# A fused attention and gated-convolution kernel: fewer tiles turned on TensorE, one store of 1/z, another order of the steps

## The chip, the cores and the metric

The kernel runs on one core of a Trainium2 chip. The metric is device time in microseconds (us), the median of several runs. Engines are called as in the profile: PE (TensorE, matmul), PEld (its weight loads), DVE (VectorE), ACT (ScalarE), POOL (GpSimd), SP (SyncE, which here issues every DMA).

## What is computed

Two layers follow each other. The first is attention of 4 batches of 12288 queries (C = 128 channels) on 768 keys that are pooled from a 384 x 32 image by 4 x 4 means and projected; keys and values are the same. The second is a causal convolution with 5 taps, a sigmoid, and two 128 x 128 projections.

```python
kv_pool = kv.reshape(B, H // r, r, W // r, r, C).mean(axis=(2, 4))
k = v = kv_pool.reshape(B, -1, C) @ w_sr
s = (1 / sqrt(C)) * (q @ k.T);  s = s - s.max(-1)
a = exp(s);  a /= a.sum(-1) + 1e-09;  x = a @ v
...
gate_pre[t] = sum(conv_w[k] * x_padded[t + k] for k in range(5))
out = (sigmoid(gate_pre) * (x @ w_val)) @ w_out
```

## The kernel before

The 4 x 12288 queries are cut into 96 groups of 512 (24 groups for each batch), and a group into 4 tiles of 128 queries (j = 0 to 3). Each group goes through these steps; names are the tiles of the profile.

Scores: for each tile six matmuls (L445) give `s` (128 x 768) from a high and a low half of q (`qh`, `ql`) and of the keys (`kh`, `kl`). DVE takes the row maximum (`nm`, L457), ACT the exponential with its row sum in `z` (L471). The result is needed with keys on the partitions, as two fp16 halves, in `pt`. There are two ways to that:

- A *straight* tile: ACT writes the high half into `hl` (L487), DVE the low half (L498), and SP issues a DMA transpose `pt<-hl` (L510). Tiles j = 0 and 1 share one DMA two tiles wide. If tile 3 is turned, tile 2 goes alone, in a DMA one tile wide.
- A *turned* tile: ACT writes the exponential into `p`, TensorE transposes it in six 128 x 128 blocks (L532) into another `s` buffer of PSUM, and ACT and DVE write the two halves from there into `pt` (L545, L549).

Which tiles are turned is said by `TURNED`; before, it is tile 3 of each group.

1/z: POOL adds 1e-9 (`ze`, L569), DVE takes the reciprocal (`r`, L573) and transposes it in 32 x 32 blocks (`rt`, L577). The four tiles' rows are stored to DRAM by four small DMAs (`rd<-rt`, L583), and read back by one DMA that spreads them over all 128 partitions (`rb<-rd`, L589), which SP issues only when the stores have landed.

Values and the rest: 18 matmuls (L610) sum `av` (one PSUM buffer) from `pt` and the value halves; DVE multiplies by 1/z into `x` (L628), which also frees `av`. POOL and ACT form the taps and the gate (L666, L677, L686), ACT the tanh (L701), PE the projections (`val` L705, `out` L714) with DVE between them (L709), ACT evacuates (L719), and SP stores two groups at a time (L739).

Buffers that matter: 3 of `s`, 1 of `av`, 4 of `hl`, 3 of `pt`, 3 of `rb`.

For each batch, `setup` loads 16 pieces of the image (`kvt`, L257, six buffers), sums them on DVE (L266), projects them (L287) and forms keys and values. The setup of batch 0 stands ahead of everything; those of batches 1 to 3 are spread among the groups of the batch ahead. `weights` loads the second layer's weights as 64-bit words (`raw`, L237) and converts them on DVE in 14 instructions (L202 to L208).

The order in which each engine, and SP, issues its instructions is fixed when the program is built: `Plan.order` simulates the engines with a duration, a due time and the buffers of each step, and takes among the steps that can begin the one due first. The hardware keeps that order on each engine; only waits remain.

Of the kernel before, what the change touches and what calls it, by code (L numbers as in the profile page):

```python
# [6 lines left out]
F32 = mybir.dt.float32  # L7
# [13 lines left out]
PERIOD = 10.4  # L21
# [11 lines left out]
class Plan:  # L33
# [3 lines left out]
    EDGE = 0.08  # L37
    DMA_LEAD, DMA_TAIL = 1.3, 0.8
# [4 lines left out]
    def pool(self, name, n):  # L43
        self.stock[name] = [(0.0, i) for i in range(n)]

    def add(self, eng, dur, due, run, after=(), takes=(), frees=(), lag=0.1, start=0.0, kind=""):
        s = Step(eng, dur, due, run, [a for a in after if a], takes, frees, lag, start, kind)
        for owner, name in frees:
            owner.users[name] = owner.users.get(name, 0) + 1
        self.steps.append(s)  # L50
        return s

    def order(self):
# [12 lines left out]
        while any(ready.values()):  # L66
            best = None
            for e, items in ready.items():
                ests = []
                for at, s in items:  # L70
                    t = max(at, free[e])
                    for name in s.takes:
                        stock = self.stock[name]
                        t = max(t, min(stock)[0]) if stock else 1e18
                    if t < 1e17:
                        ests.append((t, s))
                if not ests:
                    continue
                t0 = min(t for t, _ in ests)
                s = min((s.due + (s.kind != "" and s.kind == last[e]) * 0.3, n, s)  # L80
                        for n, (t, s) in enumerate(ests) if t <= t0 + 0.01)[2]
                if best is None or t0 < best[0]:
                    best = (t0, e, s)
            assert best, "no step can begin"
            t, e, s = best
            ready[e] = [x for x in ready[e] if x[1] is not s]
            for name in s.takes:
                stock = self.stock[name]
                pick = min(stock)
                stock.remove(pick)  # L90
                s.slot[name] = pick[1]
            if e == "SP":
                free[e] = t + 0.06
                dma = max(dma, t + self.DMA_LEAD) + s.dur
                s.end = dma + self.DMA_TAIL
            else:
                dur = s.dur
                if s.kind == "turn" and last[e] != "turn":
                    dur = s.dur / 2
                free[e] = t + dur  # L100
                s.end = t + dur + s.lag
# [21 lines left out]
def attn_moe_kernel(ctx, tc, qT, kvT, w_sr, w_moe, outT):  # L123


    nc = tc.nc
# [11 lines left out]
    T = PERIOD  # L138
    scale = 1.0 / float(C) ** 0.5
# [30 lines left out]
    pool("rd", 4, [NT, P], F32, dram)  # L170
# [39 lines left out]
    def weights():  # L210
# [26 lines left out]
        s = plan.add("SP", 1.0, 2, lambda: nc.sync.dma_start(out=raw, in_=w_moe.bitcast(I32)))  # L237
# [6 lines left out]
    def setup(b, st):  # L244
# [36 lines left out]
        for h in range(2):  # L281
            sl = slice(h * HALF, (h + 1) * HALF)

            def project(h=h, sl=sl):
                def run():
                    s.tile = tile_of(s, psum)[:, :HALF]
                    nc.tensor.matmul(s.tile, wsr, st["pool"][:, sl], start=True, stop=True)  # L287
                s = plan.add("PE", 0.64, late, run,
                             [load_sr, pools_done[(h + 1) * PIECES // 2 - 1]],
                             takes=(psum,), frees=[(holder["pool"], "pool")], lag=0.2)  # L290
                return s
# [73 lines left out]
        for h in range(2):  # L365
            sl = slice(h * HALF, (h + 1) * HALF)

            def values(h=h):
                def run():
                    s.tile = tile_of(s, psum)[:, :HALF]  # L370
                    for j in range(HALF // P):
# [4 lines left out]
                             frees=[(st["vt_by"], "vt"), (by["diag"], "diag")], lag=0.2)  # L376
# [32 lines left out]
    def group(g, prev, nxt):  # L409
# [6 lines left out]
        if g.i % 2 == 0:  # L416
# [4 lines left out]
            ld = plan.add("SP", 1.3, t0 - 4 * T, load, takes=("q",), start=t0 - 5 * T)  # L421
# [12 lines left out]
        s_qh = plan.add("ACT", 0.51, t0 - 1.5 * T, qh, [g.ld], takes=("qh",))  # L434
        s_ql = plan.add("POOL", 1.25, t0 - 1.2 * T, ql, [s_qh], takes=("ql",),
# [3 lines left out]
        def score(j):  # L439
# [8 lines left out]
            if last_of_batch:  # L448
                frees += [(st["kh_by"], "kh"), (st["kl_by"], "kl")]
            s = plan.add("PE", 1.065, t0 + j * T / 4, run, [s_qh, s_ql] + st["keys"],  # L450
                         takes=("s",), frees=frees, lag=0.2)
            return s

        def row_max(j, sc):
# [4 lines left out]
            s = plan.add("DVE", 0.87, t0 + j * T / 4 + 1.2, run, [sc], takes=("nm",))  # L459
            return s  # L460

        def expo(j, sc, mx, turned):
# [10 lines left out]
            s = plan.add("ACT", 1.02, t0 + j * T / 4 + 2.2, run, [sc, mx],  # L473
# [5 lines left out]
        def straight(j, sc, ex):  # L479
# [9 lines left out]
            s_hi = plan.add("ACT", 0.71, t0 + j * T / 4 + 3.3, hi, [ex],  # L489
# [10 lines left out]
            s_lo = plan.add("DVE", 0.865, t0 + j * T / 4 + 4.1, lo, [s_hi], frees=[(sc, "s")])  # L500
# [6 lines left out]
            def turn():  # L507
                if not g.pts:
# [5 lines left out]
            s_t = plan.add("SP", 2.1 * width, t0 + j * T / 4 + 5, turn,  # L514
                           [s_lo] if alone else [s_lo, g.los[j - 1]],
                           takes=("pt",) if j == 1 else (),
                           frees=[(g.hl_by, "hl")])
# [6 lines left out]
        def turned(j, ex):  # L524
# [3 lines left out]
            def block(k):  # L528
                def run():
                    if k == 0:  # L530
# [3 lines left out]
                s = plan.add("PE", 0.118, t0 + j * T / 4 + 3.6, run, [ex, state.get("by")],  # L534
                             takes=("s",) if k == 0 else (), frees=[(ex, "p")], lag=0.2,
                             kind="turn")
# [14 lines left out]
            s_hi = plan.add("ACT", 0.71, t0 + j * T / 4 + 4.6, hi, blocks + [g.pt_by])  # L551
            s_lo = plan.add("DVE", 0.865, t0 + j * T / 4 + 5.4, lo, [s_hi],
# [26 lines left out]
        def rd(j):  # L579
            def run():  # L580
                if j == 0:
                    g.rd = tile_of(s_rd[0], "rd")
                nc.sync.dma_start(out=g.rd[j].rearrange("(b i) -> b i", i=32),  # L583
                                  in_=g.rt[j::32, :])
            return run

        def rb():
            g.rb = tile_of(s_rb, "rb")
            nc.sync.dma_start(out=g.rb, in_=g.rd.rearrange("(o j) p -> o (j p)", o=1)  # L589
                              .broadcast_to([C, GQ]))  # L590

        s_ze = plan.add("POOL", 0.15, t0 + 1.1 * T, eps, list(g.exps.values()), takes=("ze",),
                        frees=[(g.exps[0], "z")])
        s_r = plan.add("DVE", 0.1, t0 + 1.15 * T, recip, [s_ze], takes=("r",),
                       frees=[(s_ze, "ze")])
        s_rt = plan.add("DVE", 0.1, t0 + 1.16 * T, rt, [s_r], takes=("rt",), frees=[(s_r, "r")])
        s_rd = []
        for j in range(NT):
            s_rd.append(plan.add("SP", 0.03, t0 + 1.2 * T, rd(j), [s_rt] + s_rd[:1],
                                 takes=("rd",) if j == 0 else (), frees=[(s_rt, "rt")]))  # L600
        s_rb = plan.add("SP", 1.15, t0 + 1.5 * T, rb, s_rd, takes=("rb",),
                        frees=[(s_rd[0], "rd")])


        avs = []
        for n, (name, k, a) in enumerate(AV):
            def run(n=n, name=name, k=k, a=a):
                if n == 0:
                    g.av = tile_of(avs[0], "av")
                nc.tensor.matmul(g.av, st[name][:, k * P:(k + 1) * P], g.pt[:, :, a * NCH + k],  # L610
                                 start=(n == 0), stop=(n == len(AV) - 1))
            frees = [(g.pt_by, "pt")] if n == len(AV) - 1 else []
            if n == len(AV) - 1 and last_of_batch:
                frees += [(st["vh_by"], "vh"), (st["vl_by"], "vl")]
            avs.append(plan.add("PE", 0.216, t0 + (AV_DUE + n / len(AV) * 0.9) * T, run,
                                g.ready + st["values"] + avs[-1:],
                                takes=("av",) if n == 0 else (), frees=frees,
                                lag=0.2 if n == len(AV) - 1 else -0.08))
# [13 lines left out]
        s_halo = plan.add("POOL", 0.15, t0 + (AV_DUE + 0.6) * T, halo,  # L632
# [4 lines left out]
        g.s_x = plan.add("DVE", 0.6, t0 + (AV_DUE + 0.95) * T, x, [avs[-1], s_rb, s_halo,  # L637
# [5 lines left out]
        late = t0 + (AV_DUE + 1.2) * T  # L643
# [18 lines left out]
        else:  # L662
            def act_tap(k):
# [3 lines left out]
                s = plan.add("ACT", 0.61, late - 0.1 * T + (4 - k) * 0.3 * T, run,  # L667
# [16 lines left out]
            def plus(k, tap, before):  # L684
                def run():
                    nc.gpsimd.tensor_tensor(out=g.gate, in0=g.gate, in1=tap.tile, op=ALU.add)  # L686
                return plan.add("POOL", 1.25, late, run, [tap, before],
# [33 lines left out]
        fin = t0 + (AV_DUE + 2.2) * T  # L721
        s_th = plan.add("ACT", 0.52, fin, th, [gate], takes=("th",), frees=[(gate_by, "gate")])
        s_val = plan.add("PE", 0.86, fin, val, [g.s_x, weights_done, s_th] if not tail
                         else [g.s_x, weights_done], takes=("m",),
                         frees=[(s_halo, "x")], lag=0.2)
        s_h = plan.add("DVE", 0.59, fin + 1, h, [s_val, s_th], takes=("h",),
                       frees=[(s_val, "m"), (s_th, "th")])
        s_out = plan.add("PE", 0.86, fin + 2, out, [s_h], takes=("m",), frees=[(s_h, "h")],
                         lag=0.2)
        s_ev = plan.add("ACT", 0.48, fin + 3, evac, [s_out] + ([prev.s_ev] if i else []),  # L730
# [4 lines left out]
        if tail:  # L735
            plan.add("SP", 0.7, fin + 5, lambda: nc.sync.dma_start(
                out=outT[g.b, :, g.t0:g.t0 + GQ], in_=g.o[:, i]), [s_ev], frees=[(g.o_by, "o")])
        elif i:
            plan.add("SP", 1.3, fin + 5, lambda: nc.sync.dma_start(  # L739
# [19 lines left out]
AV_DUE = 1.9  # L759
TURNED = ((3,),)  # L760
# [28 lines left out]
```

## Time and profile before

| | |
|---|---|
| median of 3 runs | 1136.8 us (1133.98 to 1137.78) |
| the profiled execution | 1133.29 us, of which the span from first to last instruction is 1131.5 us |
| busy share of the span | PE 93%, DVE 81%, POOL 78%, ACT 77%, PEld 59% |
| mean granted TensorE clock | 0.992 of 2.4 GHz |
| DMA queue | 86.4% of the 16 engines' span, 488880 packets |

Busy shares are means over the whole span. The span has three stages: a start up to about 60 us, in which the keys of batch 0 are formed and the pipeline fills, a loop from 60 to about 1100 us, and an end. An instruction's busy time overlaps that of its neighbours on PE and DVE, so what it costs in a row of others is read from the distance between starts, or from the chain that ended last.

### The profile page before, as it was taken

What the parts mean: (1) busy time and instruction counts of PE and PEld (TensorE: products, weight loads), DVE (VectorE), ACT (ScalarE), POOL (GpSimd) and SP (SyncE); (2) the same over time, 40 slices, a digit from 0 to 9 for tenths busy, and PEclk for the clock granted to TensorE, in tenths of its full rate; (3) what the DMA queues carried; (4) which work ended last, traced back from release to release, by engine and by line L of the source; (5) the groups of instructions that cost most, each with busy time, mean ns of one, the idle gap of its engine ahead of it and who ended that gap; (6) DMA issues with size and microseconds to landing.
All of it is one profiled execution on the core that took longest, in us unless ns stands there. A gap on an engine that the chain in (4) does not pass through costs nothing.

```text
span 1131.5 us, 16498 instructions
## 1 busy us (share of the span) xinstructions
PE 1050.6 (93%) x5056; PEld 667.7 (59%) x5056; DVE 918.4 (81%) x1280; ACT 869.8 (77%) x1559; POOL 884.2 (78%) x1049
## 2 busy tenths in 40 slices
PE   0799999999999999999999899999999999999996
PEld 0565656666656656666666555665666666666662
DVE  6788887878888988878888888887887788787784
ACT  1577877888777878878888777888888888887872
POOL 1167887888978788888878778888888888888872
PEclk9899999999999999999999999999999999999997
DMA  9488999888899999898999899978888898987774
GB/s 336 101 189 181 224 213 201 164 185 197 200 214 205 230 211 208 186 178 175 215 237 199 188 194 209 202 165 180 190 172 178 188 189 167 178 205 154 154 158 98
DMA packets 488968, 215.54 MB, mean 190 GB/s; under 512 B 455728, under 2 KB 455856, under 8 KB 488880
## 3 DMA queue, kind: packets, MB, share of 16 engines
q1 hardware_dynamic: 488880, 214.49, 86.4%
q8 instruction: 41, 0.67, 0.2%
q14 instruction: 47, 0.39, 0.1%
HBM read 75.83 MB, written 25.36 MB: 89 GB/s over the span
## 4 chain that ended last, share of the span: by engine, by line
PE 68%; DVE 11%; DMA 9%; SPq 4%; issue 3%; ACT 3%; POOL 1%; DVEq 0%
PE s L445 26%; PE av L610 24%; PE m L705 6%; PE m L714 6%; PE s L532 5%; DMA kvt<-in_kv 4%; DMA rb<-rd 3%; DVE nm L457 3%; SPq L510 2%; DVE hl L498 2%; DVE x L628 2%; DVE pool L266 1%; DVE pt L549 1%; SPq L583 1%; ACT s L471 1%
## 5 line engine op out<-in xcount | busy, mean ns | idle before, releaser
L686 POOL TENSOR_TENSOR gate<-gate,tap 128x512 f32<-128x512 f32 x376 | 481.6, 1281 | 14.2
L457 DVE TENSOR_REDUCE nm<-s 128x1 f32<-128x768 f32 x384 | 363.9, 951 | 79.9 <-PE s L445 77.8
L610 PE MATMUL av<-pt,vh 128*128 128x512 f16 x1152 | 374.6, 381 | 19.1 <-DVE x L628 11.9
L471 ACT ACTIVATE s<-s,nm 128x768 f32<-128x768 f32 x288 | 251.8, 874 | 111.8 <-DVE nm L457 110.6
L498 DVE SCALAR_TENSOR_TENSOR hl<-s,hl 128x768 f16<-128x768 f32 x288 | 271.8, 945 | 13.4 <-ACT hl L487 12.4
L445 PE MATMUL s<-kh,qh 128*128 128x512 f32 (+1 forms) x768 | 258.8, 418 | 19.3 <-DVE hl L498 9.6
L487 ACT ACTIVATE hl<-s 128x768 f16<-128x768 f32 x288 | 232.9, 811 | 3.8
L610 PE MATMUL av<-pt,vl 128*128 128x512 f16 x576 | 218.8, 380 | 0.0
L610 PEld LDWEIGHTS <-vh 128*128 128x128 f16 x1152 | 109.6, 98 | 179.0 <-issue 77.0
L445 PE MATMUL s<-kl,qh 128*128 128x512 f32 (+1 forms) x768 | 198.9, 340 | 0.0
L445 PE MATMUL s<-kh,ql 128*128 128x512 f32 (+1 forms) x768 | 197.6, 338 | 0.0
L677 POOL TENSOR_SCALAR tap<-x,wm 128x512 f32<-128x512 f32 x282 | 191.4, 697 | 0.1
L445 PEld LDWEIGHTS s<-kh,qh 128*128 128x128 f32 x768 | 136.9, 191 | 90.9 <-issue 21.0
L677 POOL TENSOR_SCALAR gate<-x,wm 128x512 f32<-128x512 f32 x94 | 65.4, 696 | 137.7 <-DVE x L628 137.6
L431 POOL TENSOR_TENSOR ql<-q,qh 128x512 fp32r<-128x512 f32 x96 | 122.4, 1275 | 59.8 <-ACT qh L427 59.4
L445 PEld LDWEIGHTS s<-kl,qh 128*128 128x128 f32 x768 | 118.8, 190 | 17.4 <-DVE kl L321 0.5
L445 PEld LDWEIGHTS s<-kh,ql 128*128 128x128 f32 x768 | 118.7, 190 | 17.0
L719 ACT ACTIVATE o<-m 128x512 f32<-128x512 f32 x96 | 57.4, 598 | 67.7 <-PE m L714 67.4
L549 DVE SCALAR_TENSOR_TENSOR pt<-s,pt 128x768 f16<-128x768 f32 x96 | 90.9, 947 | 20.1 <-ACT pt L545 19.8
L714 PE MATMUL m<-h,wm 128*128 128x512 f32 x192 | 100.7, 607 | 3.0 <-DVE h L709 2.0
L705 PE MATMUL m<-x,wm 128*128 128x512 f32 x192 | 99.3, 599 | 3.4 <-DVE x L628 2.7
L532 PE MATMUL s<-ident,p 128*128 128x128 f32 x576 | 96.1, 273 | 1.0 <-ACT p L471 1.0
(59 smaller groups left out, 961.2 us busy)
## 6 DMA issues: line engine op xcount, KB each, us to landing
kvt<-in_kv SPq DMA_DIRECT2D x64, 384.0 KB
q<-in_q SPq DMA_DIRECT2D x48, 512.0 KB
rb<-rd SPq DMA_DIRECT2D x96, 256.0 KB
out<-o SPq DMA_DIRECT2D x47, 512.0 KB
rd<-rt SPq DMA_DIRECT2D x384, 0.5 KB
pt<-hl SPq DMA_TRANSPOSE x192
out<-o SPq DMA_DIRECT2D x2, 256.0 KB
raw<-in_w_moe SPq DMA_DIRECT2D x1, 261.0 KB
```

The source lines that it names most:

```text
L431: nc.gpsimd.tensor_tensor(out=g.ql, in0=g.qt[:, i], in1=g.qh.bitcast(F32), op=ALU.subtract)
L445: nc.tensor.matmul(t[:, c0:c1], a[:, sl], k[:, c0:c1], start=(n == 0), stop=(n == 2))
L457: v.tensor_reduce(out=s.tile, in_=sc.tile[:, :NK], axis=AX.X, op=ALU.max, negate=True)
L471: nc.scalar.activation(out=out, in_=sc.tile[:, :NK], func=AF.Exp, bias=mx.tile, accum_out=g.z[:, j:j + 1])
L487: nc.scalar.activation(out=g.hls[j // 2][:, half, 0], in_=sc.tile[:, :NK], func=AF.Copy, scale=2.0 ** 15)
L498: v.scalar_tensor_tensor(out=hl[:, half, 1], in0=sc.tile[:, :NK], scalar=2.0 ** 15, in1=hl[:, half, 0], op0=ALU.mult, op1=ALU.subtract)
L532: nc.tensor.transpose(state["t"][:, k * P:(k + 1) * P], ex.tile[:, k * P:(k + 1) * P], ident)
L610: nc.tensor.matmul(g.av, st[name][:, k * P:(k + 1) * P], g.pt[:, :, a * NCH + k], start=(n == 0), stop=(n == len(AV) - 1))
L677: nc.gpsimd.tensor_scalar(out=s.tile, in0=src(k), scalar1=w[k], scalar2=1.0, op0=ALU.mult, op1=ALU.mult)
L686: nc.gpsimd.tensor_tensor(out=g.gate, in0=g.gate, in1=tap.tile, op=ALU.add)
L705: nc.tensor.matmul(g.m, wval, g.x[:, HALO:], start=True, stop=True)
L714: nc.tensor.matmul(g.m2, wout, g.h, start=True, stop=True)
```

## The change

It changes five things. (1) `TURNED` becomes `((3,), ())`: in even groups TensorE turns tile 3, in odd groups none; there tiles 2 and 3 go together in a second DMA two tiles wide. (2) 1/z is stored with one DMA: DVE writes the four reciprocals to columns 0, 8, 16 and 24 of `r`, the 32 x 32 transposes put them on every eighth partition, and one DMA takes 16 rows of 32 numbers. For that the queries of a group are interleaved on the host (32 of each tile in turn), and the matmuls of L610 read `pt` in runs of 32 columns, tile by tile, so that `av` comes out in the natural order. (3) The first loads of q get start times of 9, 24 and 28 us in the plan, and the load of `raw` one of 17 us, behind the loads of the keys. (4) Every due time of the group's steps is replaced by an entry of a table `DUE`, and the period by 10.29. (5) The plan's costs change: delays by engine, an issue time on SP for each DMA, a cost of going from copies to transposes, and a preference for a copy behind a copy.

```diff
-PERIOD = 10.4
+PERIOD = 10.29
+DUE = dict(q=-41.6, qh=-14.6, ql=-12.4, score=-2.1, max=2.4, exp=2.0, hi=-0.2, lo=4.1, turn=3.7,
+           pe=3.3, thi=3.1, tlo=0.3, ze=12.3, r=11.7, rt=15.3, rd=13.9, rb=9.9, av=19.8, avs=9.5,
+           halo=19.7, x=31.5, tap=32.0, gate=31.4, th=44.3, val=44.3, h=45.3, out=44.8,
+           evac=45.6, store=47.9)
...
-    EDGE = 0.08
-    DMA_LEAD, DMA_TAIL = 1.3, 0.8
+    EDGE = 0.04
+    LAG = dict(PE=0.16, ACT=0.1, DVE=0.085, POOL=0.04, SP=0.0)
+    DMA_LEAD, DMA_TAIL, CLUMP = 1.3, 0.8, 5.7
...
-                s = min((s.due + (s.kind != "" and s.kind == last[e]) * 0.3, n, s)
+                s = min((s.due - (s.kind == last[e] == "copy") * self.CLUMP, n, s)
...
-                free[e] = t + 0.06
-                dma = max(dma, t + self.DMA_LEAD) + s.dur
+                copy = s.kind == "copy"
+                free[e] = t + (0.5 if copy else 0.9 * s.dur)
+                switch = 0.6 if last[e] == "copy" and not copy else 0.0
+                dma = max(dma + switch, t + self.DMA_LEAD) + s.dur
...
-        s = plan.add("SP", 1.0, 2, lambda: nc.sync.dma_start(out=raw, in_=w_moe.bitcast(I32)))
+        s = plan.add("SP", 1.0, 2, start=17.0, run=lambda: nc.sync.dma_start(out=raw, in_=w_moe.bitcast(I32)))
...
-            ld = plan.add("SP", 1.3, t0 - 4 * T, load, takes=("q",), start=t0 - 5 * T)
+            ld = plan.add("SP", 1.3, t0 + D["q"], load, takes=("q",),
+                          start=FIRST_Q[g.i // 2] if g.i < 6 else t0 + D["q"] - T)
...
-            v.reciprocal(out=g.r[:, :NT], in_=g.ze)
+            v.reciprocal(out=g.r[:, ::32 // NT], in_=g.ze)
...
-        def rd(j):
-            def run():
-                if j == 0:
-                    g.rd = tile_of(s_rd[0], "rd")
-                nc.sync.dma_start(out=g.rd[j].rearrange("(b i) -> b i", i=32),
-                                  in_=g.rt[j::32, :])
-            return run
+        def rd():
+            g.rd = tile_of(s_rd, "rd")
+            nc.sync.dma_start(out=g.rd.rearrange("(a i) -> a i", i=32), in_=g.rt[::32 // NT, :])
...
-                nc.tensor.matmul(g.av, st[name][:, k * P:(k + 1) * P], g.pt[:, :, a * NCH + k],
+                nc.tensor.matmul(g.av, st[name][:, k * P:(k + 1) * P],
+                                 g.pt[:, :, a * NCH + k].rearrange("k j (b i) -> k b j i", i=32),
                                  start=(n == 0), stop=(n == len(AV) - 1))
...
-AV_DUE = 1.9
-TURNED = ((3,),)
+FIRST_Q = (9.0, 24.0, 28.0)
+TURNED = ((3,), ())
...
-        "in_q": np.ascontiguousarray(q.transpose(0, 2, 1)),
+        "in_q": np.ascontiguousarray(
+            q.reshape(B, N // GQ, P // 32, NT, 32, C).transpose(0, 5, 1, 3, 2, 4)
+            .reshape(B, C, N)),
```

## Rows read from the trace of the kernel before

**Rows 1.** Loop, windows: busy us of each engine, clock, DMA share, GB/s.
```profile
60.00:1100.00 1040.00, 1003.24 (x4888) 641.22 (x4887) 860.32 (x1192) 838.74 (x1505) 867.50 (x1021) 1.00 0.89 192
```

**Rows 2.** Windows, matmuls of L610 alone (18 to a group): PE and PEld busy.
```profile
600.00:720.00 120.00, 47.84 (x184) 16.53 (x183) 1.00 0.92 198
...
840.00:960.00 120.00, 53.94 (x199) 18.15 (x199) 1.00 0.90 184
...
60.00:1100.00 1040.00, 440.54 (x1675) 151.12 (x1675) 1.00 0.89 192
```

**Rows 3.** Chain that ended last, in order of time: start, us, what.
```profile
515.93 0.86 PE m L705 x2
...
517.22 0.11 PE s L532
...
517.54 1.06 PE s L445 x6
518.60 0.55 PE s L532 x5
...
519.36 0.86 PE m L714 x2
520.22 0.86 PE av L610 x4
```

**Rows 4.** Waits, whole span: who waited for whom, us in total, times, longest.
```profile
PEld L610 <- DVE x L628: 20.2, 25, 2.2
PE av L610 <- DVE x L628: 11.9, 19, 1.9
PE s L445 <- DVE hl L498: 9.6, 19, 1.7
DVE x L628 <- DMA rb<-rd: 8.3, 10, 1.7
PE av L610 <- DMA pt<-hl: 2.4, 3, 1.5
```

**Rows 5.** SP's queue in order of time: start, us, line, DMA, count.
```profile
585.32 0.52 SPq L583 DMA_DIRECT2D rd<-rt  x1
585.89 0.44 SPq L257 DMA_DIRECT2D kvt<-in_kv  x1
586.38 1.45 SPq L510 DMA_TRANSPOSE pt<-hl  x1
587.88 0.98 SPq L739 DMA_DIRECT2D out<-o  x1
588.90 1.91 SPq L583 DMA_DIRECT2D rd<-rt  x3
590.92 3.73 SPq L510 DMA_TRANSPOSE pt<-hl  x1
594.82 0.45 SPq L589 DMA_DIRECT2D rb<-rd  x1
```

**Rows 6.** Windows of 1 us in which only transposes move data.
```profile
572.00:573.00 1.00, 1.00 (x9) 0.84 (x7) 1.00 (x2) 0.97 (x3) 0.92 (x3) 1.00 1.28 290
594.00:595.00 1.00, 1.00 (x7) 0.77 (x6) 1.00 (x2) 0.32 (x3) 1.00 (x2) 1.00 1.20 217
```

**Rows 7.** The start: windows, columns as in rows 1.
```profile
0.00:25.00 25.00, 1.65 (x2) 0.50 (x2) 14.66 (x21) 3.91 (x6) 4.61 (x13) 1.00 0.94 352
25.00:60.00 35.00, 24.08 (x102) 17.69 (x103) 26.90 (x44) 18.32 (x33) 3.01 (x4) 0.90 0.51 124
```

**Rows 8.** The start: SP's queue, then DVE, then PE in order of time.
```profile
4.03 2.72 SPq L419 DMA_DIRECT2D q<-in_q  x3
...
15.47 1.31 DVE L202 TENSOR_SCALAR rest<-raw 128x261 int32<-128x261 int32 x1 [3.76 <-DMA raw<-in_w_moe]
...
27.75 0.95 DVE L266 TENSOR_REDUCE pool<-kvt 128x48 f32<-128x768 f32 x1
...
28.75 1.65 PE L287 MATMUL s<-pool,wsr 128*128 128x384 f32 x2 [8.01 <-DVE pool L266]
30.98 1.01 PE L445 MATMUL s<-kh,qh 128*128 128x512 f32 x2 [0.58 <-ACT kh L297]
```

**Rows 9.** The end, all engines in order of time.
```profile
1107.38 0.96 DVE L549 SCALAR_TENSOR_TENSOR pt<-s,pt 128x768 f16<-128x768 f32 x1
...
1107.94 1.53 SPq L510 DMA_TRANSPOSE pt<-hl  x1
...
1110.01 0.75 DVE L628 SCALAR_TENSOR_TENSOR x<-av,down,rb 128x512 f32<-128x512 f32 x1 [1.68 <-DMA rb<-rd]
...
1111.94 0.38 PE L610 MATMUL av<-pt,vh 128*128 128x512 f16 x1
```

More of the change, by code (lines that the diff above doesn't have):

```diff
@@ L44, in pool, with add @@
         self.stock[name] = [(0.0, i) for i in range(n)]
-    def add(self, eng, dur, due, run, after=(), takes=(), frees=(), lag=0.1, start=0.0, kind=""):
+    def add(self, eng, dur, due, run, after=(), takes=(), frees=(), lag=None, start=0.0, kind=""):
+        lag = self.LAG[eng] if lag is None else lag
+        if eng == "SP" and not kind:
+            kind = "copy"
         s = Step(eng, dur, due, run, [a for a in after if a], takes, frees, lag, start, kind)
@@ L92, in order @@
             if e == "SP":
-                free[e] = t + 0.06
-                dma = max(dma, t + self.DMA_LEAD) + s.dur
+                copy = s.kind == "copy"
+                free[e] = t + (0.5 if copy else 0.9 * s.dur)
+                switch = 0.6 if last[e] == "copy" and not copy else 0.0
+                dma = max(dma + switch, t + self.DMA_LEAD) + s.dur
                 s.end = dma + self.DMA_TAIL
             else:
[L97 to L101, printed above, removed]
+                free[e] = t + s.dur
+                s.end = t + s.dur + s.lag
             last[e] = s.kind
@@ L138, in attn_moe_kernel @@
     T = PERIOD
+    D = DUE
     scale = 1.0 / float(C) ** 0.5
@@ L432, in ql @@
                                     op=ALU.subtract)
-        s_qh = plan.add("ACT", 0.51, t0 - 1.5 * T, qh, [g.ld], takes=("qh",))
-        s_ql = plan.add("POOL", 1.25, t0 - 1.2 * T, ql, [s_qh], takes=("ql",),
+        s_qh = plan.add("ACT", 0.51, t0 + D["qh"], qh, [g.ld], takes=("qh",))
+        s_ql = plan.add("POOL", 1.25, t0 + D["ql"], ql, [s_qh], takes=("ql",),
                         frees=[(g.ld, "q")])
@@ L449, in score @@
                 frees += [(st["kh_by"], "kh"), (st["kl_by"], "kl")]
-            s = plan.add("PE", 1.065, t0 + j * T / 4, run, [s_qh, s_ql] + st["keys"],
-                         takes=("s",), frees=frees, lag=0.2)
+            s = plan.add("PE", 1.05, t0 + j * T / 4 + D["score"], run, [s_qh, s_ql] + st["keys"],
+                         takes=("s",), frees=frees)
             return s
@@ L458, in run @@
                                 negate=True)
-            s = plan.add("DVE", 0.87, t0 + j * T / 4 + 1.2, run, [sc], takes=("nm",))
+            s = plan.add("DVE", 0.87, t0 + j * T / 4 + D["max"], run, [sc], takes=("nm",))
             return s
@@ L472, in run @@
                                      accum_out=g.z[:, j:j + 1])
-            s = plan.add("ACT", 1.02, t0 + j * T / 4 + 2.2, run, [sc, mx],
+            s = plan.add("ACT", 0.88, t0 + j * T / 4 + D["exp"], run, [sc, mx],
                          takes=(("z",) if j == 0 else ()) + (("p",) if turned else ()),
@@ L488, in hi @@
                                      func=AF.Copy, scale=2.0 ** 15)
-            s_hi = plan.add("ACT", 0.71, t0 + j * T / 4 + 3.3, hi, [ex],
+            s_hi = plan.add("ACT", 0.71, t0 + j * T / 4 + D["hi"], hi, [ex],
                             takes=("hl",) if own else ())
@@ L499, in lo @@
                                        in1=hl[:, half, 0], op0=ALU.mult, op1=ALU.subtract)
-            s_lo = plan.add("DVE", 0.865, t0 + j * T / 4 + 4.1, lo, [s_hi], frees=[(sc, "s")])
+            s_lo = plan.add("DVE", 0.865, t0 + j * T / 4 + D["lo"], lo, [s_hi], frees=[(sc, "s")])
             g.los[j] = s_lo
@@ L513, in turn @@
                 g.pts.append(s_t)
-            s_t = plan.add("SP", 2.1 * width, t0 + j * T / 4 + 5, turn,
+            s_t = plan.add("SP", 1.85 * width, t0 + j * T / 4 + D["turn"], turn,
                            [s_lo] if alone else [s_lo, g.los[j - 1]],
                            takes=("pt",) if j == 1 else (),
-                           frees=[(g.hl_by, "hl")])
+                           frees=[(g.hl_by, "hl")], kind="turn")
             if j == 1:
@@ L533, in run @@
                                         ex.tile[:, k * P:(k + 1) * P], ident)
-                s = plan.add("PE", 0.118, t0 + j * T / 4 + 3.6, run, [ex, state.get("by")],
-                             takes=("s",) if k == 0 else (), frees=[(ex, "p")], lag=0.2,
-                             kind="turn")
+                s = plan.add("PE", 0.109, t0 + j * T / 4 + D["pe"], run, [ex, state.get("by")],
+                             takes=("s",) if k == 0 else (), frees=[(ex, "p")])
                 if k == 0:
@@ L550, in lo @@
                                        in1=flat(0), op0=ALU.mult, op1=ALU.subtract)
-            s_hi = plan.add("ACT", 0.71, t0 + j * T / 4 + 4.6, hi, blocks + [g.pt_by])
-            s_lo = plan.add("DVE", 0.865, t0 + j * T / 4 + 5.4, lo, [s_hi],
+            s_hi = plan.add("ACT", 0.71, t0 + j * T / 4 + D["thi"], hi, blocks + [g.pt_by])
+            s_lo = plan.add("DVE", 0.865, t0 + j * T / 4 + D["tlo"], lo, [s_hi],
                             frees=[(blocks[0], "s")])
@@ L577, in rt @@
             v.transpose(out=g.rt, in_=g.r)
[L579 to L585 removed]
+        def rd():
+            g.rd = tile_of(s_rd, "rd")
+            nc.sync.dma_start(out=g.rd.rearrange("(a i) -> a i", i=32), in_=g.rt[::32 // NT, :])
         def rb():
             g.rb = tile_of(s_rb, "rb")
[L589 removed]
+            nc.sync.dma_start(out=g.rb, in_=g.rd.rearrange("(o q) -> o q", o=1)
                               .broadcast_to([C, GQ]))
[L592 removed]
+        s_ze = plan.add("POOL", 0.28, t0 + D["ze"], eps, list(g.exps.values()), takes=("ze",),
                         frees=[(g.exps[0], "z")])
[L594 removed]
+        s_r = plan.add("DVE", 0.1, t0 + D["r"], recip, [s_ze], takes=("r",),
                        frees=[(s_ze, "ze")])
[L596 to L602, printed above, removed]
+        s_rt = plan.add("DVE", 0.1, t0 + D["rt"], rt, [s_r], takes=("rt",), frees=[(s_r, "r")])
+        s_rd = plan.add("SP", 0.03, t0 + D["rd"], rd, [s_rt], takes=("rd",),
+                        frees=[(s_rt, "rt")])
+        s_rb = plan.add("SP", 0.8, t0 + D["rb"], rb, [s_rd], takes=("rb",),
+                        frees=[(s_rd, "rd")])
         avs = []
@@ L631, in group @@
         cont = prev is not None and prev.b == g.b
-        s_halo = plan.add("POOL", 0.15, t0 + (AV_DUE + 0.6) * T, halo,
+        s_halo = plan.add("POOL", 0.15, t0 + D["halo"], halo,
                           [prev.s_x] if cont else [], takes=("x",),
@@ L636, in group @@
         g.s_halo = s_halo
-        g.s_x = plan.add("DVE", 0.6, t0 + (AV_DUE + 0.95) * T, x, [avs[-1], s_rb, s_halo,
+        g.s_x = plan.add("DVE", 0.66, t0 + D["x"], x, [avs[-1], s_rb, s_halo,
                                                                    st["down_by"]],
@@ L666, in run @@
                     nc.scalar.activation(out=s.tile, in_=src(k), func=AF.Copy, scale=w[k])
-                s = plan.add("ACT", 0.61, late - 0.1 * T + (4 - k) * 0.3 * T, run,
+                s = plan.add("ACT", 0.61, t0 + D["tap"], run,
                              [g.s_x, weights_done], takes=(f"tap{k}",), frees=[(s_halo, "x")])
@@ L686, in run @@
                     nc.gpsimd.tensor_tensor(out=g.gate, in0=g.gate, in1=tap.tile, op=ALU.add)
-                return plan.add("POOL", 1.25, late, run, [tap, before],
+                return plan.add("POOL", 1.3, late, run, [tap, before],
                                 frees=[(tap, f"tap{k}")])
```

31 lines of the change are left out of this document (15 added, 16 removed).

## The prediction

> **What bounds the kernel now.** I read the windows of the loop first. Between 60 and 1100 us PE is busy for 1003.2 of 1040 us at the full clock, POOL for 868, DVE for 860 and ACT for 839 [rows 1]. 1675 matmuls of L610 at 18 to a group are 93.06 groups, so the pace is 1040 / 93.06 = 11.18 us a group [rows 2]. The chain of waits shows that PE really is at work: instructions of PE follow each other without a hole, and its pieces give the cost of each kind in a full queue: six score matmuls 1.06 us, four of L610 0.86 us (0.215 each), each of the two projections 0.86 us, and the six blocks of a turned tile 0.11 + 0.55 = 0.66 us [rows 3]. A group therefore needs 4 x 1.06 + 18 x 0.215 + 2 x 0.86 + 0.66 = 10.49 us of PE, 94% of the pace. The remaining 37 us of PE idle in the loop (1040 - 1003.2) are many small waits: for `x`, which frees the one `av` buffer (20.2 + 11.9 us, which overlap in part), for low halves (9.6 us), hardly any for a transposed tile (2.4 us in 3 waits) [rows 4]. So in the loop PE sets the pace. At the start it does not: the first score comes at 30.98 us, and what ends the wait for it is DVE's summing of the image [rows 8].
>
> **The change part by part.** The sum is made against the profiled execution, 1133.3 us (span 1131.5 and 1.8 around it), which stands 3.5 us below the median of the runs shown; the prediction carries over to a median within that.
>
> *Turning.* 48 tiles leave TensorE: 48 x 0.66 us = **-31.7 us** if PE keeps setting the pace [rows 3]. ACT and DVE do the same work for a tile either way (an exponential, a high and a low half). What is added is 48 tiles by DMA: one two-wide transpose in place of a one-wide one. On SP's queue that is 3.73 against 1.45 us, 2.28 us more in each odd group [rows 5]. On the DMA engines a tile (128 x 1536 fp16, 393 KB) takes 393 / 290 = 1.36 us to 393 / 217 = 1.81 us [rows 6]. The work that must hide this is the other traffic's slack: the DMA share of the loop is already 0.89 [rows 1]. I cost it at nothing, since a transposed tile is almost never what the value matmuls wait for [rows 4]; if that cover is gone, it costs up to 48 x 1.81 = +87 us (rival B).
>
> In an odd group tile 3's low half is now followed by a DMA and not by PE, so the last of `pt` comes some 4 us later after its scores; its users, L610, are due 19.8 us after the group's start, before and after, so three `pt` buffers have to carry the delay. I take nothing.
>
> *One store of 1/z.* Before, four stores cost SP 0.52 + 1.91 = 2.43 us a group; one costs about 0.5 [rows 5]. This takes 1.9 us a group off SP's queue, more than the 2.28 / 2 = 1.14 us a group that the transposes add, so SP ends with 0.8 us a group less. What is queued behind the stores is the read back `rb`, then `x`, then the next group's L610, where PE waits now [rows 4]. A gain is possible but is not counted here; it is a part of the order below. `r` and `rt` keep their instruction counts.
>
> *L610 reading in runs of 32 columns.* No row shows such a read. Bounds: nothing, or, if each matmul ran like four separate 128-column ones at the 0.11 us of L532, 0.44 against 0.215 us, +4 us a group [rows 3]. I take nothing: each run is 64 contiguous bytes of the same partition, and the tile is the one that L610 reads today in runs of 128 columns at full rate. The Trainium skill, "SBUF — State Buffer", in its note on cachelines, says that reads keep full bandwidth while at least two accesses fall in one 16-byte line; by it too the term would be zero, and no run here shows it yet.
>
> *Keys first.* In the first 25 us the queue moves 352 GB/s x 25 us = 8.8 MB [rows 7]: 16 image pieces (6.3 MB) with four loads of q (2.1 MB) and `raw` among them. DVE stands 3.76 us for `raw`, and its conversions lie between the sums; the sixteenth sum ends at 28.7 us and the projection follows at 28.75 [rows 8]. With only one load of q among them, 6.3 + 0.5 + 0.1 = 6.9 MB at 352 GB/s take 19.6 us, and the last sum ends about 1.5 us later, at 21 to 22 us: 7 us earlier. The conversions are then owed between 25 and 60 us, where DVE is busy for 26.9 of 35 us [rows 7]; 14 instructions of 0.3 to 1.3 us are about 5 us, for which I charge 1.5. Term: **-5.5 us** (bounds -8 and 0).
>
> *The end.* The last group is odd, so its tile 3 ends in a two-wide DMA. Before, tile 2's narrow one goes out at 1107.94, beside tile 3's last half (1107.38 to 1108.34), and L610 begins at 1111.94 [rows 9]. A two-wide one can only start then and takes 2.28 us longer [rows 5]. **+2 us** (bounds 0 and +4).
>
> *The order and the plan's costs.* Nothing is added or removed, but every queue changes. Bounds from the kernel's own paces: the best 120 us of the loop hold 199 matmuls of L610, 10.85 us a group, the worst 184, 11.74 us [rows 2]. Held for 96 groups these are -32 and +54 us. I take 0, the mean pace; between the ends nothing singles out another value.
>
> Sum: 1133.3 - 31.7 - 5.5 + 2 = 1098.1; I say **1097 us**.
>
> **The rivals.**
>
> *A, the forecast:* PE goes on setting the pace, the loop falls to about 10.85 us a group. 1076 to 1114 us.
>
> *B, the other side: the DMA engines become the bound.* The place is L610 waiting for `pt<-hl`. The loop has 0.89 x 1040 = 926 us of DMA time [rows 1]; 48 x 1.81 = 87 us more make 1013, which PE's shortened loop (1040 - 31.7 = 1008) no longer holds. If the share cannot rise above 0.95, the loop is 1013 / 0.95 = 1066 us, and the time 1133.3 + 26 - 5.5 + 2 = 1156. It decides against the change as soon as an extra tile costs more than (31.7 + 3.5) / 48 = 0.73 us that nothing covers. For it: that share. Against it: the share counts packets' time and passes 1 when transposes alone move (1.28 at 290 GB/s, 1.20 at 217), so the same bytes occupy the engines longer or shorter as they are fed [rows 6]; and L610 waits 2.4 us for it in all now [rows 4]. The Trainium skill, "VectorE: DVE Perf Modes", rules for kernel authors, advises TensorE for a 128 x 128 transpose where PSUM may be its destination and the DMA crossbar otherwise; that rule speaks against this change and for B. The trace agrees on the price of one tile taken alone (0.66 us on PE, at least 1.36 us by DMA), not on which is scarce.
>
> *C: PE's time is freed, but the others take it.* POOL, DVE and ACT are at 839 to 868 us of 1040 [rows 1], and with a loop of 1008 at 83 to 86%; more small waits than today eat most of the 31.7 us. About 10 us of it are left: 1133.3 - 10 - 5.5 + 2 = 1120; none of it: 1130.
>
> *D: the new order also removes about half of PE's 37 us of idle time,* as earlier stores and reads of 1/z shorten the wait for `x`: 1098 - 18 = 1080, or less, down to 1065.
>
> **How the numbers follow.** A 0.58, B 0.14, C 0.14, D 0.14. The prediction is A's. The range leaves out the greater part of B and the far end of D: 1067 to 1133 us. A difference under 0.3% (3.4 us) can't be told from no change in this kernel. A and D are faster, of C most (0.11): 0.83. Within 0.3%: a little of B and C, 0.05. Slower: 0.12.
>
> **What would show it.** L532 falls from 576 to 288 matmuls and `rd<-rt` from 384 to 96 DMAs. A: the loop's pace near 10.85 us, PE still at 95% or more, 0.215 us for each L610 in the chain. Keys first: first score at 23 to 25 us and not at 31. B: waits of L610 for `pt<-hl` grow from 2.4 to 30 us or more, with the DMA share at 0.95. C: PE's idle time in the loop well over 37 us, its releasers DVE and ACT. D: the waits for `x` well under 20 us. The forecast is wrong if an L610 takes over 0.22 us in a full queue, or if `pt` comes late.

## The result, and the profile after

| | before | changed |
|---|---|---|
| median | 1135.4 us (1132.1 to 1137.8, 4 runs) | 1092.0 us (1089.1 to 1094.4, 4 runs) |
| the profiled execution | 1133.3 us, span 1131.5 | 1094.4 us, span 1092.6 |

The ratio is 0.9618, 95% interval 0.9582 to 0.9655: 3.8% faster, 43 us. The forecast was 1097 us with a range of 1067 to 1133 us.

The loop, in windows of the changed kernel (busy us of PE, PEld, DVE, ACT and POOL, clock, DMA share, GB/s), answers to [rows 1]:

```profile
60.00:1060.00 1000.00, 963.79 (x4570) 607.08 (x4570) 848.22 (x1185) 830.54 (x1492) 861.96 (x1012) 0.99 1.03 217
```

PE is as busy as before (96%), with fewer instructions; the DMA share rose from 0.89 to 1.03 and the rate from 192 to 217 GB/s. The value matmuls alone, L610 before and L614 now, answer to [rows 2]:

```profile
60.00:720.00 660.00, 282.86 (x1079) 100.17 (x1079) 0.99 1.05 223
...
720.00:1060.00 340.00, 150.66 (x582) 54.20 (x583) 1.00 1.01 204
60.00:1060.00 1000.00, 433.52 (x1661) 154.37 (x1662) 0.99 1.03 217
```

1661 / 18 = 92.3 groups in 1000 us are 10.84 us a group, where 11.18 stood before and 10.85 was forecast. But the pace is uneven: 11.01 us a group up to 720 us, while the image pieces of batches 1 to 3 are loaded, and 10.52 after that. The kernel before was uneven too: 11.34 and 10.93 in the same two windows (1048 and 560 matmuls).

The chain that ended last, from two stretches of the changed kernel, prices the kinds of work in a full queue, as [rows 3] did:

```profile
638.10 0.55 PE s L543 x5
```

```profile
1027.28 1.74 PE av L614 x8
1029.02 1.05 PE s L456 x6
1030.07 0.86 PE m L710 x2
```

Eight value matmuls take 1.74 us, 0.2175 each, against 0.215 before; over the whole of both traces the median distance between the starts of neighbouring value matmuls is the same, 0.216 us. Reading `pt` in runs of 32 columns costs nothing that can be seen. The waits of the changed kernel (us in total, times, longest), which answer to [rows 4]:

```profile
PE s L456 <- DVE hl L509: 30.4, 37, 2.7
...
PE av L614 <- DVE x L633: 4.3, 4, 1.8
...
PEld L614 <- DMA pt<-hl: 2.6, 4, 1.1
...
PEld L614 <- DVE x L633: 2.1, 1, 2.1
...
PE av L614 <- DMA pt<-hl: 1.4, 4, 0.4
```

The wait of the value matmuls for `x` has gone from 20.2 + 11.9 to 2.1 + 4.3 us, and that for a transposed tile stays small. What took its place is scores that wait for an `s` buffer (9.6 before, 30.4 now). SP's queue in order of time, against [rows 5]:

```profile
499.70 3.68 SPq L521 DMA_TRANSPOSE pt<-hl  x1
503.43 0.57 SPq L595 DMA_DIRECT2D rb<-rd  x1
504.10 0.39 SPq L429 DMA_DIRECT2D q<-in_q  x1
504.73 0.48 SPq L591 DMA_DIRECT2D rd<-rt  x1
505.26 1.51 SPq L521 DMA_TRANSPOSE pt<-hl  x1
510.06 0.33 SPq L595 DMA_DIRECT2D rb<-rd  x1
510.49 4.35 SPq L521 DMA_TRANSPOSE pt<-hl  x1
```

One store of 0.48 us stands where 0.52 + 1.91 us stood. The start, against [rows 8], and the end, against [rows 9], all in order of time:

```profile
24.83 1.65 PE L297 MATMUL s<-pool,wsr 128*128 128x384 f32 x2 [9.43 <-DVE pool L276]
27.05 1.01 PE L456 MATMUL s<-kh,qh 128*128 128x512 f32 x2 [0.58 <-ACT kh L307]
```

```profile
1069.20 4.38 SPq L521 DMA_TRANSPOSE pt<-hl  x1
```

The first score comes 3.9 us earlier than before. From the issue of the last transpose to the end of the span there are 23.4 us now (1092.6 - 1069.2) and 23.6 before (1131.5 - 1107.94).

### The profile page after: what moved, and what is told of

Its sections match the earlier page's. It is cut to its first block, busy times and chain, and to the rows that moved or that the text cites. A ratio compares the mean times of both kernels' runs of the same rounds, so it can differ in the third digit from the quotient of the medians.

```text
span 1092.6 us, 15687 instructions
## 1 busy us (share of the span) xinstructions
PE 1016.0 (93%) x4768; PEld 636.8 (58%) x4768; DVE 914.4 (84%) x1280; ACT 868.8 (80%) x1559; POOL 887.2 (81%) x1049
## 4 chain that ended last, share of the span: by engine, by line
PE 55%; DVE 15%; DMA 13%; ACT 11%; issue 4%; SPq 2%; POOL 0%; DVEq 0%; ACTq 0%
PE s L456 24%; PE av L614 20%; DMA kvt<-in_kv 12%; DVE nm L468 5%; DVE hl L509 5%; PE m L719 5%; PE m L710 5%; ACT s L482 5%; ACT hl L498 3%; DVE pt L559 2%; PE s L543 1%; DMA pt<-hl 1%; ACT tap L671 1%; ACT pt L555 1%; DVE pool L276 1%
## 5 line engine op out<-in xcount | busy, mean ns | idle before, releaser
L614 PE MATMUL av<-pt,vh 128*128 128x512 f16 x1152 | 379.8, 383 | 5.6 <-DVE x L633 4.3
L482 ACT ACTIVATE s<-s,nm 128x768 f32<-128x768 f32 x336 | 293.9, 875 | 90.2 <-DVE nm L468 89.5
L509 DVE SCALAR_TENSOR_TENSOR hl<-s,hl 128x768 f16<-128x768 f32 x336 | 318.3, 949 | 31.7 <-ACT hl L498 27.2
L456 PE MATMUL s<-kh,qh 128*128 128x512 f32 (+1 forms) x768 | 261.3, 421 | 35.5 <-DVE hl L509 30.4
L498 ACT ACTIVATE hl<-s 128x768 f16<-128x768 f32 x336 | 271.6, 810 | 4.3
L614 PE MATMUL av<-pt,vl 128*128 128x512 f16 x576 | 220.3, 382 | 0.0
L614 PEld LDWEIGHTS <-vh 128*128 128x128 f16 x1152 | 112.9, 98 | 166.7 <-issue 82.9
L456 PEld LDWEIGHTS s<-kh,qh 128*128 128x128 f32 x768 | 139.7, 192 | 101.8 <-issue 38.0
L614 PEld LDWEIGHTS <-vl 128*128 128x128 f16 x576 | 56.7, 98 | 87.7 <-issue 54.3
L276 DVE TENSOR_REDUCE pool<-kvt 128x48 f32<-128x768 f32 x64 | 60.5, 946 | 42.6 <-DMA kvt<-in_kv 41.2
L633 DVE SCALAR_TENSOR_TENSOR x<-av,down,rb 128x512 f32<-128x512 f32 x96 | 71.3, 742 | 3.2 <-PE av L614 3.2
```

The costliest lines, as they stand in the source:

```text
L276: v.tensor_reduce(out=st["pool"][:, i * PC:(i + 1) * PC], in_=ld.tile.rearrange("c (k s) -> c k s", s=RR), axis=AX.X, op=ALU.add)
L456: nc.tensor.matmul(t[:, c0:c1], a[:, sl], k[:, c0:c1], start=(n == 0), stop=(n == 2))
L482: nc.scalar.activation(out=out, in_=sc.tile[:, :NK], func=AF.Exp, bias=mx.tile, accum_out=g.z[:, j:j + 1])
L498: nc.scalar.activation(out=g.hls[j // 2][:, half, 0], in_=sc.tile[:, :NK], func=AF.Copy, scale=2.0 ** 15)
L509: v.scalar_tensor_tensor(out=hl[:, half, 1], in0=sc.tile[:, :NK], scalar=2.0 ** 15, in1=hl[:, half, 0], op0=ALU.mult, op1=ALU.subtract)
```

## The experiments

The question left by this trace is which of the five edits made the 43 us, and whether TensorE's share of them is the 31.7 us of the forecast. Ratios below are to the kernel before, run on the same chip. The runs come from several chips, on which the kernel before had medians of 1131.8 to 1136.6 us; a difference in us between two runs is therefore good to some 4 us, and where that matters the ratios stand beside it.

**TensorE turns tile 3 in every group again.**

```diff
-TURNED = ((3,), ())
+TURNED = ((3,),)
```

> The changed kernel, but TensorE turns tile 3 in every group again; order, costs, start and single store as changed. Theory A (TensorE sets the pace, and its 48 turned tiles are what went away): 48 x 0.66 = 31.7 us come back, less the 2 us of the end: about 1121 us, loop pace near 11.17 us a group. Rival (the gain is from the new order and the single store, and turning fewer tiles is eaten by the DMA queue): 1092 to 1100 us.

Measured: 1125.0 us, ratio 0.9933 (0.9908 to 0.9958). Beside 1092.0 us that is 33 us for 48 tiles, 0.69 us a tile; by the two ratios (0.9933 and 0.9618) it is 36 us, 0.75 a tile. Within the intervals of the ratios that is the forecast's term, 0.66. Four of the five edits together leave only 0.7%.

**Only the turned tiles changed, in the kernel before.**

```diff
-TURNED = ((3,),)
+TURNED = ((3,), ())
```

> The kernel before with only the turned tiles changed: tile 3 is turned in even groups alone. Theory A: 1135 - 31.7 + 2 = about 1106 us. Rival (with four stores of 1/z and the old order SP's queue and the DMA engines can't take 48 more tiles): 1130 us or more, with waits of the value matmuls for pt<-hl well over 2.4 us.

Measured: 1186.8 us, ratio 1.0477 (1.0437 to 1.0517). The same 48 tiles that give 33 to 36 us in the changed kernel cost 55 us here (the kernel before took 1131.8 us on this chip). The rival's time is right, its place is not: the waits, whole span, are

```profile
DVE x L628 <- DMA rb<-rd: 32.5, 29, 3.7
PE av L610 <- DVE x L628: 28.4, 39, 3.0
PEld L610 <- DVE x L628: 21.2, 18, 3.3
PE av L610 <- DMA pt<-hl: 5.9, 4, 2.7
```

`rb` comes late (8.3 us of waits before, 32.5 now), `x` with it, and `av` is held. Neither theory had `rb`. That it is late because longer transposes stand in front of its stores on SP's queue is argued from the queue's order; the next two runs test whether SP's time is what runs short, in the changed kernel.

**Four stores of 1/z in the changed kernel.** The old store, arrangement of q and matmul reads; order planned anew.

```diff
-        s_rd = plan.add("SP", 0.03, t0 + D["rd"], rd, [s_rt], takes=("rd",),
-                        frees=[(s_rt, "rt")])
+        s_rd = []
+        for j in range(NT):
+            s_rd.append(plan.add("SP", 0.03, t0 + D["rd"], rd(j), [s_rt] + s_rd[:1],
+                                 takes=("rd",) if j == 0 else (), frees=[(s_rt, "rt")]))
```

> The changed kernel, but 1/z is stored by four DMAs again (queries and matmul reads in the old arrangement); turned tiles, due times, costs and start as changed. Prediction's step (the store is worth nothing by itself): 1088 to 1097 us. Rival (the store's time on SP is what makes room for the 48 tiles): 1.9 us a group more on a queue that is 85 to 87% taken fills it, so 1110 us or more.

Measured: 1172.5 us, ratio 1.0351 (1.0305 to 1.0396). The rival holds. Since the order also differs, the next run keeps it.

**Four DMAs for the one store, same order on every engine.**

```diff
-            nc.sync.dma_start(out=g.rd.rearrange("(a i) -> a i", i=32), in_=g.rt[::32 // NT, :])
+            out = g.rd.rearrange("(a i) -> a i", i=32)
+            for n in range(NT):
+                nc.sync.dma_start(out=out[n * NT:(n + 1) * NT], in_=g.rt[32 * n:32 * n + 32:32 // NT, :])
```

> The changed kernel with the very same order on every engine, but the one store of 1/z is issued as four DMAs of four rows one behind the other: the same 16 runs of 128 bytes, 1.5 us more of SP's time a group. Theory (SP's issue time is what the four stores cost, and what has no room beside 48 more transposes): 1130 to 1175 us, DMA share below that of the changed kernel. Rival (the kernel with four stores was slow for its other order): 1090 to 1100 us.

Measured: 1202.9 us, ratio 1.0584 (1.0543 to 1.0626), 111 us more than the changed kernel, or 1.16 us a group, for three more DMAs a group and not one byte. The theory holds against its rival, but its range ends 28 us too low. SP's queue, the loop's window and two of the waits:

```profile
505.53 0.44 SPq L597 DMA_DIRECT2D rb<-rd  x1
506.08 0.36 SPq L429 DMA_DIRECT2D q<-in_q  x1
506.53 2.42 SPq L593 DMA_DIRECT2D rd<-rt  x4
508.99 5.52 SPq L521 DMA_TRANSPOSE pt<-hl  x2
514.69 0.45 SPq L597 DMA_DIRECT2D rb<-rd  x1
```

```profile
60.00:1060.00 1000.00, 895.28 (x4127) 557.16 (x4126) 774.74 (x1077) 755.41 (x1352) 781.45 (x916) 0.97 0.92 198
```

```profile
PE av L616 <- DMA pt<-hl: 38.5, 28, 3.9
PEld L616 <- DMA pt<-hl: 15.7, 12, 2.7
```

The queue hardly pauses, and yet the DMA engines do less than in the changed kernel (0.92 against 1.03): they are not fed. Adding up the durations of SP's DMA instructions from 60 to 1060 us gives 83% of the time before, 86% in the changed kernel and 93% here. SP's DMAs for the store of a group take 2.43 us in the mean here and 0.62 there, 1.8 us more and not 1.5; those for a transpose take the same, 3.8 us. SP's queue, not the bytes, is what the four stores use up. The clock may add to it: the mean granted clock of the whole run is 0.962, against 0.992 in the changed kernel. By an estimate from the missing shares and the spans (0.038 x 1205.6 less 0.008 x 1092.6), that is at most 37 us; no run separates it from the waits.

**The single store alone, in the kernel before** (edit 2, with the arrangement of q and the matmul reads that go with it).

```diff
-            v.reciprocal(out=g.r[:, :NT], in_=g.ze)
+            v.reciprocal(out=g.r[:, ::32 // NT], in_=g.ze)
...
+            nc.sync.dma_start(out=g.rd.rearrange("(a i) -> a i", i=32), in_=g.rt[::32 // NT, :])
```

> The kernel before with only the single store of 1/z (interleaved queries, value matmuls reading in runs of 32 columns); the old order, costs and turned tiles. Prediction's step (nothing by itself, reading in runs of 32 costs nothing): 1128 to 1137 us and 0.215 us for each value matmul in a full queue. Rival (SP's queue held TensorE up by late 1/z): 1120 us or less. If the runs of 32 cost something: above 1145 us.

Measured: 1123.7 us, ratio 0.9884 (0.9839 to 0.9928), 12 to 13 us faster, between the two expectations. Its waits for `x`, against [rows 4]:

```profile
PEld L604 <- DVE x L623: 5.2, 10, 0.8
...
PE av L604 <- DVE x L623: 2.1, 6, 0.6
```

They fall from 20.2 + 11.9 to 5.2 + 2.1 us: with SP's queue shorter, 1/z is there in time.

**Single store and half the turned tiles, old order.** As in the last run, and `TURNED = ((3,), ())`.

```diff
-TURNED = ((3,),)
+TURNED = ((3,), ())
```

> The kernel before with two of the five changes: the single store of 1/z and no turned tile in odd groups; old order, old costs, old start. Theory (the single store makes room on SP's queue, then TensorE's 31.7 us can be had; order and start are worth nothing): 1124 - 31.7 = about 1092 us. Rival (the new order with SP's issue times in the plan is needed too): 1110 us or more.

Measured: 1136.4 us, ratio 0.9987 (0.9956 to 1.0018). The theory falls: with the store the 48 tiles no longer cost 55 us, but 12 to 13, and they still give nothing. This is the run that shows that something of the new order is needed. Its waits:

```profile
PE av L604 <- DMA pt<-hl: 12.0, 12, 2.7
...
PEld L604 <- DMA pt<-hl: 9.9, 9, 3.5
```

22 us of waits for transposed tiles, where the changed kernel has 4.

**The same, with the value matmuls later in the order.**

```diff
-AV_DUE = 1.9
+AV_DUE = 2.2
```

> The kernel before with the single store and no turned tile in odd groups, as in the run that came out at 1136 us, and AV_DUE 2.2 in place of 1.9: the value matmuls and all behind them stand 3.1 us later in the order against scores and transposes. Theory (what the new order adds is time between a tile's transpose and its value matmuls: scores, high halves and transposes are due 1.3 to 3.5 us earlier in it, the value matmuls at the same time): the waits for pt<-hl, 22 us in that run, fall under 8 us, and the time to 1095 to 1115 us. Rival (it is the issue times of SP in the plan): 1128 us or more.

Measured: 1097.7 us, ratio 0.9654 (0.9600 to 0.9707), and its waits:

```profile
PEld L604 <- DMA pt<-hl: 1.2, 1, 1.2
PE av L604 <- DMA pt<-hl: 1.2, 3, 0.5
```

One number of the old order, 3.1 us more in the plan between a group's transposes and its value matmuls (with all that stands behind them), takes 39 us off and brings the kernel before, with the store and the turned tiles, to within 6 us of the changed one. The traces show the distance as well: in the odd groups from 9 to 89, where no tile is turned, the mean time from the issue of a group's last transpose to its first value matmul is 7.7 us in the run at 1136 us, 8.8 here and 9.6 in the changed kernel, while that from the first score to the first value matmul stays at 25.2 to 25.7 us. So that distance is what the new order supplies; its costs for SP and its preference for copies in a row are not needed for most of the gain.

**No tile turned.**

```diff
-TURNED = ((3,), ())
+TURNED = ((),)
```

> The changed kernel, but no tile is turned on TensorE. If TensorE still set the pace: 1092 - 31.7 = 1060 us. If the DMA engines are full (their share in the loop is already 1.03): 48 more tiles of 1.36 to 1.81 us are 65 to 87 us that nothing covers, so 1125 us or more, and the value matmuls wait for pt<-hl for tens of us.

Measured: 1179.9 us, ratio 1.0420 (1.0386 to 1.0453). The DMA side is the bound here: its share is 1.04, PE is busy for 891 of 1000 us, and the value matmuls wait for tiles:

```profile
60.00:1060.00 1000.00, 890.88 (x3943) 535.53 (x3943) 794.00 (x1096) 768.62 (x1377) 792.55 (x931) 0.97 1.04 219
```

```profile
PE av L614 <- DMA pt<-hl: 32.6, 21, 3.9
PEld L614 <- DMA pt<-hl: 22.1, 21, 3.2
```

48 more tiles cost 88 us, 1.83 us each (91 us by the ratios), near the upper price of [rows 6]; at the 219 GB/s of this window their 18.9 MB alone would take 86 us, by an estimate. Whether the DMA engines or SP's queue give the bound is not separated: SP's DMA instructions fill 95% of the window, and the clock is lower too (0.967 over the run). Rival B is real, one step further on.

**The image pieces of batches 1 to 3 cut to a sixteenth, same order.**

```diff
-                nc.sync.dma_start(out=t, in_=kvT[b, i])
+                n = PC * RR if first else PC
+                nc.sync.dma_start(out=t[:, :n], in_=kvT[b, i][:, :n])
...
-                                in_=ld.tile.rearrange("c (k s) -> c k s", s=RR),
+                                in_=ld.tile.rearrange("c (k s) -> c k s", s=RR) if first else
+                                ld.tile[:, :PC].rearrange("c (k o) -> c k o", o=1)
+                                .broadcast_to([C, PC, RR]),
```

> The changed kernel with the same order, but in batches 1 to 3 only the first 48 of the 768 columns of each image piece are loaded, and DVE's sum reads these 48 sixteen times over (same elements read, so the batch's keys are not the reference's): 17.7 MB less to move. Theory (the stretch with these loads is slow, 11.0 against 10.5 us a group, because the DMA engines are full there): the stretch falls to 10.5 us a group, 1062 to 1070 us. Rival (it is slow for DVE's 48 sums and PE's projections): 1085 to 1092 us.

Measured: 1066.5 us, ratio 0.9386 (0.9358 to 0.9414). The value matmuls in two stretches:

```profile
60.00:720.00 660.00, 291.58 (x1125) 103.40 (x1125) 1.00 1.00 207
720.00:1060.00 340.00, 149.95 (x585) 54.54 (x585) 1.00 0.97 197
```

1125 in place of 1079: the first stretch falls from 11.01 to 10.56 us a group and is about as fast as the second. With 17.7 MB less to move, the same order and sums that take DVE as long as before (0.94 against 0.95 us), 25 us are gone: up to 720 us the changed kernel is held by its DMA traffic.

**DVE's sums of the pieces later.**

```diff
-                         frees=[(ld, "kvt")], start=at(i))
+                         frees=[(ld, "kvt")], start=at(i) if first else at(i) + LATE)
...
+LATE = 10.0
```

> The changed kernel, but in batches 1 to 3 DVE's sums of the image pieces may begin 10 us later in the plan than now, so that they stand behind their loads; the same work and bytes. In the changed kernel the stretch with these loads runs at 10.9 us a group and the one without at 10.4. If DVE's in-order wait for a late piece (33 us in the loop) is the cause: 1070 to 1080 us and these waits under 10 us. If the stretch is slow for the bytes and DVE's time themselves: 1089 to 1095 us.

Measured: 1095.9 us, ratio 0.9645 (0.9610 to 0.9680). DVE's waits for pieces fall from 41.2 to 20.1 us over the whole span, and nothing is won. Only half of the waits went, and the order was planned anew; but with the run before, this speaks for the wait as a sign of the full DMA engines and not as the cause.

**The start.** In the kernel before, only the start times:

```diff
-        s = plan.add("SP", 1.0, 2, lambda: nc.sync.dma_start(out=raw, in_=w_moe.bitcast(I32)))
+        s = plan.add("SP", 1.0, 2, start=17.0, run=lambda: nc.sync.dma_start(out=raw, in_=w_moe.bitcast(I32)))
...
-            ld = plan.add("SP", 1.3, t0 - 4 * T, load, takes=("q",), start=t0 - 5 * T)
+            ld = plan.add("SP", 1.3, t0 - 4 * T, load, takes=("q",),
+                          start=FIRST_Q[g.i // 2] if g.i < 6 else t0 - 5 * T)
...
+FIRST_Q = (9.0, 24.0, 28.0)
```

> The kernel before with only the start times of the first loads of q and of raw changed. The trace of the changed kernel has its first score 3.9 us earlier, so: 1131 us, first score near 27 us. If the start is given back later in the pipeline's filling: 1135 us. By the prediction's own 5.5 us: 1130 us.

Measured: 1134.2 us, ratio 0.9992 (0.9965 to 1.0020). First score at 25.9 us, 5.1 us earlier, and no change of time. The windows of its value matmuls from 0 to 240 us hold 301 against 297 before (0.2 groups, 2.5 us ahead), those from 0 to 480 us 674 against 684: what the start gives is lost in the loop. And in the changed kernel, the load of q for groups 6 and 7, which goes out ahead of the last pieces, moved behind them:

```diff
-                          start=FIRST_Q[g.i // 2] if g.i < 6 else t0 + D["q"] - T)
+                          start=FIRST_Q[g.i // 2] if g.i < 8 else t0 + D["q"] - T)
...
-FIRST_Q = (9.0, 24.0, 28.0)
+FIRST_Q = (9.0, 24.0, 28.0, 40.0)
```

> The changed kernel, but the load of q for groups 6 and 7, which went out ahead of the last five pieces of the keys, gets a start time of 40 us. Its 0.52 MB at 350 GB/s are 1.5 us: first score at 25.5 and not 27.05 us, 1090.5 us in all. Rival: the six buffers of the image pieces pace the start, not the bytes: first score stays at 27 us.

Measured: 1098.3 us, ratio 0.9666 (0.9620 to 0.9713). First score at 24.5 us, 2.5 us earlier, and no gain either. Both runs also got another order for the whole kernel, since every due step after the start is placed anew; a difference of a few us between two such runs can be that alone.

## Why the number came out, and where its reasons did not

The table has the times in us and, in brackets, the ratios to the kernel before on the same chip.

| 1/z stores, order | tile 3 turned in every group | in every second group |
|---|---|---|
| four, old | 1135 (1) | 1187 (1.048) |
| four, new | not run | 1172 (1.035) |
| one, old | 1124 (0.988) | 1136 (0.999) |
| one, old, values 3.1 us later | not run | 1098 (0.965) |
| one, new | 1125 (0.993) | **1092** (0.962) |

*Turning, -31.7 us.* Right in the changed kernel: 33 to 36 us. PE is 96% busy in the loop and the prices of its work held to about 1%. But PE does not set the pace alone, as the forecast had it: up to 720 us the DMA traffic holds the changed kernel, and with the image pieces cut it is 25 us faster. And the step "I cost it at nothing, since a transposed tile is almost never what the value matmuls wait for" failed as it stood. That wait was small in the trace before because the transposes there had room; it said nothing of how much. In the kernel before the 48 tiles cost 55 us, with one store 12 to 13 us, and they give 33 to 36 us only with the store and the distance.

*One store, taken as 0.* Mis-sized: 12 to 13 us by itself. The prediction had named the mechanism (SP's queue, then `rb`, `x`, the next value matmuls) and declined to price it. For turning half the tiles it decides the sign: in the new order 1092 us with one store, 1172 with four. The sign that it gave for rival D came too, waits for `x` of 6.4 us in all, but the scores' waits for `s` rose by 21 us. Its balance of SP's queue did not hold: not 0.8 us a group less, but 9.3 us of SP's time a group before and after (830 and 860 us from 60 to 1060 us, for 89.3 and 92.3 groups), as the issue of the transposes grew by 1.7 us a group and not 1.14.

*The order, taken as 0.* Right with every tile 3 turned (0.993 against 0.988, intervals just overlap), wrong with half: 42 to 44 us between 1136 and 1092. And "three `pt` buffers have to carry the delay. I take nothing" was the place: due times of the value matmuls did not move, but those of scores, high halves and transposes moved 1.3 to 3.5 us ahead, and this distance is what the later transposes needed.

*Keys first, -5.5 us.* The first score did come earlier, by 3.9 us and not 7, because two loads of q went out ahead of the last pieces and not one; with one, in the last run above, it came 6.5 us earlier than before. No run shows that it shortens the whole.

*Runs of 32 columns, 0, and the end, +2 us.* 0.216 us from start to start in both traces, and 23.4 against 23.6 us from the last transpose to the end: nothing either way.

So the sum was 1133.3 - 31.7 - 5.5 + 2 = 1098, while the measured parts are about -12 for the store, -33 to -36 for turning, and near 0 for start and end: 1085 to 1088, against 1094 in the profiled execution and 1092 in the median. The closeness of the number is in part luck: the store left out (12 us) and the start and end counted in (3.5 us) offset each other in part; and the two covers that the turning needs, the store and the distance, were in the same change. Rival B was weighed as an alternative to the forecast; the runs show it to be the forecast's condition.

Left open: whether the four stores cost SP's issue time alone, or whether small DMAs also delay the transposes behind them in the queue. The experiment with the same order adds both; that a transpose holds SP for 3.8 us in the mean with and without the four DMAs speaks for the first, but does not show when the data landed. A kernel that turns more tiles while the image pieces are loaded and fewer afterwards was not tried.

## What to carry to other kernels

Work that is moved from a full engine to DMA must find room in three places: the engines' bandwidth, the issuing queue's time, and the distance in the order between the DMA and its user. A short wait for that DMA in the old trace shows that today's load fits, not that more does; add up the issuing queue's durations before and after. Edits whose effects depend on each other can't be priced one by one against the kernel before: price the cover with the edit that uses it.

## What was not expected of the hardware

Three more small DMAs a group, with the same bytes in the same 128-byte runs and the same order, cost 1.16 us a group where SP's time for them grew by 1.8 us, at a DMA share that fell from 1.03 to 0.92 (a part of the 1.16 us can be the lower clock). And the DMA share alone does not say whether DMA holds the kernel: it is 1.03 in the changed loop with PE 96% busy and 1.04 with no tile turned and PE 89% busy; and up to 720 us, at 1.05 and with PE 95% busy, 17.7 MB less to move took 25 us off.
